# The first products of layer 1 become a kind of their own in the planner of an attention and two-layer kernel

## The chip, the cores and the metric

The kernel runs on one core of one Trainium2 chip. The metric is the device time of one execution in microseconds (us). Three runs of the kernel before took 815.68, 815.87 and 816.68 us; the median is 815.87 us. The traces come from one further, profiled execution.

## The reference

Four batches of eight heads of causal attention over 576 tokens of width 64, with a decay between positions, feed two dense layers over 2304 tokens, all in float32:

```
scores = scale * q @ k.T + (cum[i] - cum[j]),  cum = cumsum(log(clip(f, 1e-4, 1)));  causal
attn   = softmax(scores);   x = attn @ v             # 2304 x 512
h = x @ w_in                                         # layer 1, 512 -> 1024
solu = h * softmax(h);  ln = (solu - mean) / sqrt(var + 1e-6) * g_ln
x = ln @ w_out                                       # 1024 -> 512
h = max(x @ w2_in, 0);  out = (h * h) @ w2_out       # layer 2, 512 -> 2048 -> 512
```

## The kernel before, in words

**Stages.** Attention walks over 20 query tiles (up to 128 rows each, a tile of 64 rows in every batch), and over 8 heads in each. For a head TensorE (PE) makes the scores in a PSUM bank `z` (L567, two matmuls; four for the widest rows, then with both banks), VectorE (DVE) finds the row's least value (L588), ScalarE (ACT) takes the exponential into one of three buffers `adj` (L602), PE transposes it through a rotating PSUM bank `pp` (L621), ACT or DVE copies that to `pt` (L376, L382), and PE multiplies it with `v` into `xo` (L641). When a tile is done its rows are scaled and transposed (L667).

**Layer 1** runs beside attention. Whenever 128 tokens are ready, `first` (L845 on) issues for such a block eight steps of *first products*, three matmuls each: L860, L861, L862, 512 columns, low and high parts of `x` and `w_in`, accumulated in the two banks `hp`. A chain then normalises the block: DVE maximum (L873), ACT exponential (L878), DVE product (L883), ACT square, which overwrites `hp` (L899), POOL scaling into `e` (L921). PE transposes `e` (L938), and `out1` multiplies by `w_out` (L811 to L813). The next block's first products may only write `hp` when L899 is through with it. There are 18 blocks, so 144 such steps. ACT, DVE and POOL also prepare the weights of both layers meanwhile (`convert`, L699 on, and `early2`, L1089 to L1105).

**Layer 2** follows (L1332, L1383, L1484 to L1486), a stretch of dense matmuls that starts at 448.4 us of the span.

**What sets the order.** Nothing is scheduled on the chip: the program's order on each engine is written out by `Plan.lay` (L127 on), a list scheduler that runs when the kernel is built. Each step has a duration per engine, a priority (lower is more urgent) and dependences; `LAT` gives the delay from one engine to another. A step that several engines can do, such as a copy, goes where it ends first. For PE a step also has a *kind*: `r` for ordinary products, `h` for scores of 64 rows, `t` for transposes, `c` for the attention's products with `v`. `TURN` (L48) is the time in ns that the plan adds when PE goes from one kind to another: `tr=86` is from transposes to products. The choice among PE's candidates counts that time, and adds HOLD = 1000 to the priority number of a candidate whose kind is not that of the step before, so that equal kinds stay together. A pair that `TURN` does not list costs nothing. The first products, the products of `out1` and all of layer 2 have the default kind `r`.

**Filler.** Where the plan sees a gap of more than 400 ns on PE before 140 us of its own time (GAP, WARM), it puts in transposes of the identity whose result nobody reads: as many as 60% of the gap takes at 62 ns each (`fill`, L102; `filler`, L1693).

Of the kernel before, what the change touches and what calls it, by code (L numbers as in the profile page):

```python
# [27 lines left out]
class Plan:  # L28
# [10 lines left out]
        pe=dict(pe=0, dve=196, act=215, pool=200, dma=1100),  # L39
# [5 lines left out]

    TICK, DUTY = 10240 / 3, 1280.0

    TURN = dict(rt=20, tr=86, rc=93, tc=94, cr=250, ct=200, th=60, ht=100, rh=20, hr=10, hc=20, ch=200)  # L48

    def __init__(self, slots, banks):  # L50
        self.banks = banks
# [75 lines left out]
    def lay(self, slack=60):  # L127
# [11 lines left out]
        def pe_end(t, ns, mark):  # L139
            k = int(t // self.TICK)  # L140
            while True:
                rate = 1.0 if work.get(k - 1, 0.0) >= self.DUTY else 0.5
                room = max(0.0, (k + 1) * self.TICK - t)
                if ns <= room * rate:
                    if mark:
                        work[k] = work.get(k, 0.0) + ns
                    return t + ns / rate
                if mark:
                    work[k] = work.get(k, 0.0) + room * rate
                ns -= room * rate  # L150
                k += 1
                t = k * self.TICK
# [28 lines left out]
        while todo:  # L181
            pick = None
            for e in engs:
# [21 lines left out]
                if e == "pe":  # L205

                    turn = {x[1]: self.TURN.get(kind + x[1].kind, 0) for x in cand}
                    t0 = min(x[0] + turn[x[1]] for x in cand)
# [37 lines left out]
            if e == "pe":  # L246
                pe_end(t, s.eng[e] + self.TURN.get(kind + s.kind, 0), True)
                kind = s.kind
# [20 lines left out]
def tile_kernel(ctx: ExitStack, tc: tile.TileContext, q, k, v, f, w_in, w_out, g_ln, w2_in, w2_out, out):  # L269
# [8 lines left out]
    KC = DM // P  # L278
# [161 lines left out]
    def slot_time(s):  # L440
        return when[s] if s < len(when) else TEND + (s - len(when)) * 2000
# [403 lines left out]
    def first(x):  # L845

        n0 = xs_done[x]
        a = slot_time(H * (n0 + 1) + LAG)
        b = slot_time(H * (xs_done[x + 1] + 1) + LAG) if x + 1 < NTT else a + EACH * TAILR
        d = b - a  # L850
# [4 lines left out]
        xk = [(nm, i, o) for nm in ("xh", "xl") for o in offs]  # L855
        for c in range(2):
            w = slice(c * 512, c * 512 + 512)
            for cc in range(KC):
                def fn(c=c, cc=cc, w=w):
                    nc.tensor.matmul(HP[:, c], lhsT=XL[i][:, cc, :], rhs=wih[:, cc, w], start=(cc == 0), stop=False)  # L860
                    nc.tensor.matmul(HP[:, c], lhsT=XH[i][:, cc, :], rhs=wil[:, cc, w], start=False, stop=False)  # L861
                    nc.tensor.matmul(HP[:, c], lhsT=XH[i][:, cc, :], rhs=wih[:, cc, w], start=False, stop=(cc == KC - 1))  # L862

                pl.add(
                    dict(pe=693), fn, a + d * FH * (c * KC + cc) / 8, xk + [("wi", cc, c, y) for y in "hl"], ["h"]
                )

        t1 = a + d * FH
# [1 line left out]
        hf = HP.rearrange("p a x -> p (a x)")  # L870
# [118 lines left out]
    def carve(tag, sizes, dt=F32R, old=None):  # L989

        memo = {}
        out, o = [], 0
        for n in sizes:
            def get(o=o, n=n):
                if "t" not in memo:
                    memo["t"] = new(tag, [sum(sizes)], dt)
                return memo["t"][:, o : o + n]

            out.append((get, held[tag] if old is None else old))
            o += n  # L1000
        return out
# [18 lines left out]
    c = carve("woh", [512] * 7 + [256] * 2)  # L1020
# [8 lines left out]
    c = carve("q2", [512] * 4)  # L1029
# [606 lines left out]
    for n in range(NQ):  # L1636
        for h in range(H):
            s = n * H + h
            if h == 0 and n + 2 < NQ:
                load_v(n + 2, when[s])  # L1640
            if h == PK and n + 1 < NQ:
                prep_k(n + 1, when[s])
                if n + 2 < NQ:
                    load_k(n + 2, when[s])
            if h == PQ and n + 1 < NQ:
                prep_q(n + 1, when[s])
                if n + 2 < NQ:
                    load_q(n + 2, when[s])
            head(s)
            w = 4 if n >= QUADS else 2  # L1650
            if (h + 1) % w == 0:
                mix(s, w)
        if tiles[n]["done"]:
            first(tiles[n]["x"])
# [60 lines left out]
FH, FO = 0.25, 0.7  # L1715
# [64 lines left out]
```

## Time and profile before

| what | value |
|---|---|
| median of three runs | 815.87 us |
| the profiled execution | 816.74 us |
| its span, first to last instruction | 814.9 us |
| PE busy | 796.5 us, 98% of the span |
| PE weight loads busy | 730.9 us, 90% |
| DVE, ACT, POOL busy | 636.8, 544.4, 392.2 us |
| DMA | 159.69 MB, 196 GB/s on average |

A busy time is the union of an engine's instructions, and the ends of matmuls are modelled; so PE's work is better read from the distance between the starts of matmuls that follow each other. Filler counts as busy too.

### The profile page before, as it was taken

Reading aid. Unit: us, or ns where it says so; the run is one execution under the profiler, and the core shown is the slowest. Engines: PE = TensorE matmul, PEld = TensorE weight load, DVE = VectorE, ACT = ScalarE, POOL = GpSimd, SP = SyncE. Lnnn points to the kernel's source line nnn. Section 1 sums busy time; section 2 is a strip of 40 time slices with the busy share of each in tenths; the row PEclk is TensorE's granted clock in tenths of the full one; section 3 lists DMA queues with packets and bytes.
Section 4 is the critical chain, followed back from the end, with each engine's and each line's share of the span. In section 5 each row is a group of like instructions: output and inputs, shape, how many; then the busy total and the mean of one; then the engine's idle time right before and its main releaser. Section 6 shows DMA issues by size and latency. Waiting matters only on the chain.

```text
span 814.9 us, 19217 instructions
## 1 busy us (share of the span) xinstructions
PE 796.5 (98%) x6648; PEld 730.9 (90%) x6648; DVE 636.8 (78%) x1626; ACT 544.4 (67%) x1405; POOL 392.2 (48%) x541
## 2 busy tenths in 40 slices
PE   8899999999999999999999999999999999999997
PEld 7677777888888888888889999999999999999997
DVE  8898777878977677677678888789779877987776
ACT  6899988888898888899787765444335433533332
POOL 6467766767678875688767522120211121112110
PEclk9999999999999999999999999999999999999999
DMA  6744336666665455666577899697667767666401
GB/s 198 224 135 131 105 104 189 189 181 198 193 197 192 147 190 172 192 214 197 170 234 245 258 324 371 205 316 228 209 210 240 233 190 245 200 221 189 149 18 36
DMA packets 109665, 159.69 MB, mean 196 GB/s; under 512 B 12832, under 2 KB 52768, under 8 KB 109568
## 3 DMA queue, kind: packets, MB, share of 16 engines
q1 hardware_dynamic: 109568, 158.47, 61.5%
q8 instruction: 52, 0.85, 0.5%
q14 instruction: 45, 0.37, 0.1%
HBM read 121.65 MB, written 36.72 MB: 194 GB/s over the span
## 4 chain that ended last, share of the span: by engine, by line
PE 56%; ACT 3%; DVE 3%; DMA 2%; issue 2%; POOL 1%; DVEq 0%; SPq 0%; POOLq 0%; ACTq 0%
PE z L1383 9%; PE pp L1383 9%; PE hp L1484 3%; PE hp L1486 3%; PE hp L1485 3%; PE z L1332 3%; PE pp L621 2%; PE pp L811 2%; PE z L567 2%; PE xo L1484 2%; PE xo L1486 2%; PE xo L1485 2%; PE pp L812 2%; PE pp L813 2%; PE hp L860 1%
## 5 line engine op out<-in xcount | busy, mean ns | idle before, releaser
L602 ACT ACTIVATE adj<-z,st 64x288 f32<-64x288 f32 (+9 forms) x192 | 95.4, 501 | 17.3 <-DVE st L588 16.4
L567 PE MATMUL z<-k,q 128*128 128x256 f32 (+17 forms) x384 | 89.9, 332 | 0.9 <-ACT adj L602 0.8
L588 DVE CUSTOM_DVE_ANT_0 z<-z,maskb 128x128 f32<-128x128 f32 (+8 forms) x144 | 65.2, 463 | 29.2 <-PE z L567 26.7
L621 PE MATMUL pp<-ident,adj 128*128 128x128 f32 (+1 forms) x480 | 76.2, 274 | 6.1 <-ACT adj L602 4.9
L812 PE MATMUL pp<-ln,wol 128*128 128x256 f32 x288 | 80.2, 278 | 0.0
L813 PE MATMUL pp<-ln,woh 128*128 128x256 f32 x288 | 80.1, 278 | 0.0
L376 ACT COPY pt<-pp 128x256 f32<-128x256 f32 (+5 forms) x169 | 67.4, 420 | 16.5 <-PE pp L621 15.6
L621 PEld LDWEIGHTS pp<-ident,adj 128*128 128x128 f32 (+1 forms) x480 | 50.5, 140 | 30.8 <-ACT adj L602 19.3
L1144 DVE TENSOR_TENSOR k<-adj,k 128x512 fp32r<-128x512 f32 x72 | 50.5, 701 | 32.9 <-POOL k L380 24.9
L380 POOL TENSOR_SCALAR k<-adj 128x512 fp32r<-128x512 f32 x41 | 25.6, 624 | 85.0 <-PE xo L1486 31.7
L734 POOL TENSOR_TENSOR free<-free 128x256 uint32<-128x256 uint32 x64 | 50.4, 794 | 31.0 <-DVE free L728 25.0
L641 PE MATMUL xo<-pt,vn 128*64 128x128 f32 (+1 forms) x960 | 61.3, 268 | 0.6 <-ACT pt L376 0.3
L567 PEld LDWEIGHTS z<-k,q 128*128 128x128 f32 (+3 forms) x384 | 54.8, 177 | 7.6 <-ACT adj L602 3.8
L860 PE MATMUL hp<-wih,xl 128*128 128x512 f32 x144 | 60.3, 419 | 0.8 <-ACT hp L899 0.8
L641 PEld LDWEIGHTS xo<-pt,vn 128*64 128x64 f32 x960 | 49.0, 137 | 11.3 <-issue 6.1
L861 PE MATMUL hp<-wil,xh 128*128 128x512 f32 x144 | 56.6, 393 | 0.2 <-DVE wil L738 0.2
L862 PE MATMUL hp<-wih,xh 128*128 128x512 f32 x144 | 56.7, 393 | 0.0
L812 PEld LDWEIGHTS pp<-ln,wol 128*128 128x128 f32 x288 | 54.4, 189 | 0.5
L813 PEld LDWEIGHTS pp<-ln,woh 128*128 128x128 f32 x288 | 54.2, 188 | 0.0
L1097 POOL TENSOR_TENSOR free<-free 128x256 f32<-128x256 f32 x64 | 51.8, 810 | 3.7 <-DMA w2f<-free 1.2
L1383 PE MATMUL z<-wol,k 128*128 128x256 f32 x384 | 52.5, 276 | 0.0
L1089 POOL TENSOR_TENSOR free<-free 128x256 fp32r<-128x256 f32 x63 | 48.3, 781 | 8.4 <-ACT free L376 7.5
(576 smaller groups left out, 2688.5 us busy)
## 6 DMA issues: line engine op xcount, KB each, us to landing
k<-w2u SPq DMA_DIRECT2D x96, 256.0 KB
ln<-w2u SPq DMA_DIRECT2D x96, 256.0 KB
w2u<-free SPq DMA_DIRECT2D x56, 256.0 KB
kn<-in_k_dram SPq DMA_DIRECT2D x32, 256.0 KB
free<-in_moe_w_out_dram SPq DMA_DIRECT2D x32, 256.0 KB
free<-in_moe_w_in_dram SPq DMA_DIRECT2D x32, 256.0 KB
q<-w2u SPq DMA_DIRECT2D x32, 256.0 KB
w2f<-free SPq DMA_DIRECT2D x49, 128.0 KB
```

The source lines that it names most:

```text
L376: nc.scalar.copy(dst(), src())
L567: nc.tensor.matmul(dst, lhsT=ql[0:r, p, 0:m], rhs=rhs, start=(g == 0), stop=(g == 1))
L588: nc.vector.tensor_tensor_reduce(out=z, in0=z, in1=maskb[0:m, o : o + e - a], scale=1.0, scalar=st[0:m, 0:1] if y else 3e38, op0=ALU.add, ...
L602: nc.scalar.activation(out=adj[0:m, c[1] : c[2]], in_=Z[c[0]][0:m, 0 : c[2] - c[1]], func=AF.Exp, bias=st[0:m, low : low + 1], scale=-1.0, ...
L621: nc.tensor.transpose(at(sk)[:, (c - g) * m : (c - g + 1) * m], adj[0:m, zc : zc + P], ident[0:m, 0:m])
L641: nc.tensor.matmul(XO[own[j], g // 2, off : off + m], lhsT=VN[vslot[b, c]][:, (g + j) * D : (g + j + 1) * D], rhs=PT[(s - h + g + j) % NPT ...
L812: nc.tensor.matmul(px, lhsT=wol[:, fc, w], rhs=hi, start=False, stop=False)
L813: nc.tensor.matmul(px, lhsT=woh[:, fc, w], rhs=hi, start=False, stop=(fc == KF - 1))
L860: nc.tensor.matmul(HP[:, c], lhsT=XL[i][:, cc, :], rhs=wih[:, cc, w], start=(cc == 0), stop=False)
L861: nc.tensor.matmul(HP[:, c], lhsT=XH[i][:, cc, :], rhs=wil[:, cc, w], start=False, stop=False)
L862: nc.tensor.matmul(HP[:, c], lhsT=XH[i][:, cc, :], rhs=wih[:, cc, w], start=False, stop=(cc == KC - 1))
L1383: nc.tensor.matmul(half(i), lhsT=l, rhs=r[:, c * TB : c * TB + TB], start=(j == start), stop=(j == 5), skip_group_check=True,)
```

## The change

`TURN` gets seven pairs with a new kind `f`, and the step of the first products is given that kind. A pair with `f` that is not listed (`fr`) costs nothing. Since these steps are no longer of kind `r`, HOLD now also stands between them and scores, `out1` and layer 2, in both directions.

```
-    TURN = dict(rt=20, tr=86, rc=93, tc=94, cr=250, ct=200, th=60, ht=100, rh=20, hr=10, hc=20, ch=200)
+    TURN = dict(rt=20, tr=86, rc=93, tc=94, cr=250, ct=200, th=60, ht=100, rh=20, hr=10, hc=20, ch=200,
+        rf=85, tf=110, cf=200, hf=85, ft=100, fc=93, fh=20)
...
                 pl.add(
-                    dict(pe=693), fn, a + d * FH * (c * KC + cc) / 8, xk + [("wi", cc, c, y) for y in "hl"], ["h"]
+                    dict(pe=693), fn, a + d * FH * (c * KC + cc) / 8, xk + [("wi", cc, c, y) for y in "hl"], ["h"],
+                    kind="f",
                 )
```

The arithmetic is the same; the built program differs in its order on all five engines. Line numbers of the changed kernel are one or two higher (L860 is L861, L938 is L940). On PE every matmul of the program is there as often as before, except the filler: 256 transposes of the identity before, 225 now. The first 63 rows of PE's order are the same, and after row 2597 of 4238, early in layer 2, nothing differs. Runs of first products without another kind between them are 86 before and 55 now; runs of at least six steps are one before and seven now. Changes between the groups L567 at 128 rows, L567 at 64 rows, transposes, L641, first products, `out1` and layer 2 number 529 before and 484 now.

On PE, in the fifth query tile (64 rows, 576 columns), between two heads. `hp` takes first products, `z` scores, `adj` is transposed for a head, `e` for a block of layer 1. Before:

```order
L621 MATMUL pp_127<-ident_110,adj_26_97 128x64 x5
L567 MATMUL z_122<-k_45_116,q_41_112 64x288
L567 MATMUL z_122<-k_7_78,q_20_91 64x288
L1693 MATMUL pp_126<-ident_110 128x128 x13
L567 MATMUL z_121<-k_45_116,q_41_112 64x288
L567 MATMUL z_121<-k_7_78,q_20_91 64x288
L938 MATMUL pp_126<-ident_110,e_90 128x128 x4
L621 MATMUL pp_125<-ident_110,adj_28_99 128x64 x5
L938 MATMUL pp_127<-ident_110,e_90 128x128 x4
```

The same place in the changed kernel:

```order
L622 MATMUL pp_127<-ident_110,adj_26_97 128x64 x5
L861 MATMUL hp<-wih_74,xl_38_109 128x512
L862 MATMUL hp<-wil_75,xh_37_108 128x512
L863 MATMUL hp<-wih_74,xh_37_108 128x512
L940 MATMUL pp_125<-ident_110,e_90 128x128 x4
L940 MATMUL pp_126<-ident_110,e_90 128x128 x4
L568 MATMUL z_121<-k_45_116,q_41_112 64x288
L568 MATMUL z_121<-k_7_78,q_20_91 64x288
```

The scores of this head stand earlier now, a step of first products and both transposes of `e` stand where 13 filler transposes stood.

On PE, in the fifteenth query tile (64 rows, 576 columns), at the first step of the 13th block of layer 1. `hp` is again the bank of the first products. Before, the transposes of `e` of the 12th block stand ahead of it:

```order
L567 MATMUL z_122<-k_46_117,q_42_113 64x288
L567 MATMUL z_122<-k_8_79,q_20_91 64x288
L621 MATMUL pp_127<-ident_110,adj_28_99 128x64 x5
L938 MATMUL pp_126<-ident_110,e_90 128x128 x4
L938 MATMUL pp_125<-ident_110,e_90 128x128 x4
L860 MATMUL hp<-wih_74,xl_38_109 128x512
L861 MATMUL hp<-wil_75,xh_37_108 128x512
```

The same step in the changed kernel:

```order
L568 MATMUL z_122<-k_46_117,q_42_113 64x288
L568 MATMUL z_122<-k_8_79,q_20_91 64x288
L622 MATMUL pp_126<-ident_110,adj_28_99 128x64 x5
L861 MATMUL hp<-wih_74,xl_38_109 128x512
L862 MATMUL hp<-wil_75,xh_37_108 128x512
```

The block now begins before `e` of the block ahead is transposed. From the last first product of the 12th block to this row PE's order has, in the changed kernel, 20 matmuls of L642 (the trace shows each of this kind twice), transposes of one head, the four score matmuls of a head, 12 products of `out1`, four score matmuls more and the transposes shown.

## Rows read from the trace of the kernel before

**Rows 1.** Windows by stage: busy us (count) of PE, PEld, DVE, ACT, POOL; clock, DMA.

```profile
38.00:88.00 50.00, 47.79 (x351) 37.83 (x351) 41.81 (x95) 48.28 (x118) 34.85 (x45) 1.00 0.44 134
73.80:143.60 69.80, 66.86 (x554) 53.29 (x552) 52.80 (x147) 62.46 (x189) 50.58 (x69) 1.00 0.44 131
143.60:448.40 304.80, 300.34 (x2445) 260.52 (x2444) 228.00 (x601) 261.14 (x735) 221.72 (x299) 1.00 0.62 194
448.40:792.00 343.60, 343.60 (x3014) 343.60 (x3013) 276.83 (x697) 152.70 (x318) 70.89 (x110) 1.00 0.70 225
```

**Rows 2.** Waits of PE in the stretch 143.6 to 448.4: us, times, longest.

```profile
PE pp L621 <- ACT adj L602: 1.9, 6, 0.5
```

**Rows 3.** Timeline of PE, 92 to 101: start, us, instruction; filler, then `out1`.

```profile
94.99 1.58 PE L1693 MATMUL pp<-ident 128*128 128x128 f32 x13
96.44 0.48 PE L567 MATMUL z<-k,q 128*64 128x288 f32 x2
...
100.16 0.28 PE L812 MATMUL pp<-ln,wol 128*128 128x256 f32 x1
...
100.98 0.28 PE L813 MATMUL pp<-ln,woh 128*128 128x256 f32 x1
```

**Rows 4.** Timeline of PE, 112 to 126: changes of kind.

```profile
114.62 0.39 PE L862 MATMUL hp<-wih,xh 128*128 128x512 f32 x1
114.85 0.80 PE L567 MATMUL z<-k,q 128*64 128x288 f32 x4
115.58 0.52 PE L621 MATMUL pp<-ident,adj 64*128 64x64 f32 x5
116.03 0.66 PE L938 MATMUL pp<-ident,e 128*128 128x128 f32 x4
116.44 0.48 PE L860 MATMUL hp<-wih,xl 128*128 128x512 f32 x1
116.76 0.39 PE L861 MATMUL hp<-wil,xh 128*128 128x512 f32 x1
116.99 0.40 PE L862 MATMUL hp<-wih,xh 128*128 128x512 f32 x1
117.31 0.80 PE L641 MATMUL xo<-pt,vn 128*64 128x64 f32 x20
118.05 0.52 PE L621 MATMUL pp<-ident,adj 64*128 64x64 f32 x5
...
118.91 0.78 PE L567 MATMUL z<-k,q 128*64 128x288 f32 x4
119.53 0.39 PE L860 MATMUL hp<-wih,xl 128*128 128x512 f32 x1
```

**Rows 5.** Timeline, 152.6 to 162.7: one block, from last first product to transposes.

```profile
152.81 0.39 PE L862 MATMUL hp<-wih,xh 128*128 128x512 f32 x1
...
157.51 1.21 ACT L899 ACTIVATE hp<-e,sm 128x1024 f32<-128x1024 f32 x1 [0.46 <-DVE sm L893]
...
162.32 0.55 PE L938 MATMUL pp<-ident,e 128*128 128x128 f32 x3 [0.24 <-POOL e L921]
```

**Rows 6.** Timeline, 296 to 301: a head's scores and its transposes.

```profile
296.16 0.71 PE L567 MATMUL z<-k,q 128*128 128x512 f32 x2
...
299.81 0.66 PE L621 MATMUL pp<-ident,adj 128*128 128x128 f32 x4 [0.39 <-ACT adj L602]
```

**Rows 7.** Waits of SP, which issues the DMAs: us, times, longest.

```profile
SPq L1372 <- PE pp L1383: 71.8, 72, 2.8
SPq L1372 <- PE z L1383: 70.9, 71, 2.8
```

**Rows 8.** Windows of PE alone near start and end: busy, clock, DMA share, GB/s.

```profile
2.00:6.00 4.00, 4.00 (x20) 1.00 0.81 266
8.00:10.00 2.00, 2.00 (x21) 1.00 0.48 76
810.00:815.00 5.00, 0.23 (x2) 0.84 0.31 105
```

## The prediction

> **What bounds the kernel now.** I read the windows by stage first. From 448.4 us on PE is busy for 343.60 of 343.60 us, and its order there changes only up to row 2597, early in that stage; so layer 2 costs what it did, and a gain or loss in attention reaches the end whole, if layer 2's inputs come earlier too. In attention there are two regimes [rows 1]. From 38 to 88 us ACT is busy for 48.28 of 50 us: ACT is the bound, and PE, at 47.79, holds filler. From 143.6 to 448.4 us PE is busy for 300.34 of 304.80 us while ACT has 261.14 and DVE 228.00: PE is the bound, and only its matmuls, the changes between their kinds and some 4.5 us of waits count. Next I read PE's waits there, mostly transposes that wait for the exponential: 1.9 us, six times [rows 2]. Last I read the timeline, for what filler and a change of kind cost.
>
> **Filler that goes.** 31 of the 256 filler transposes are gone. 13 of them hold PE from 94.99 until the scores start at 96.44, 1.45 us, with no idle time behind them, so one takes 0.11 us [rows 3]. All 31: 3.4 us. By the order, PE's matmuls without filler up to the first scores of the eighth tile (143.6 us before) are exactly the same ones in both kernels; if PE waits no more than before, it gets there 3.4 us earlier. What decides is ACT. It has 62.46 us of work in the 69.80 from 73.8 to 143.6, and by the order only two instructions more up to that point (277 for 275, shares of the copies moving both ways). In 66.4 us that is 94%, and 38 to 88 us shows that 97% can be held [rows 1]. Nearer in, from the fourth tile's first exponential to the middle of the fifth tile, ACT has 87 instructions for 98 before; the weight preparation that left comes later, where ACT has gaps. So the gaps are really smaller, not only left unfilled. Bounds: the whole 3.4 us comes back, or none, if idle time takes the filler's place. I take -3.4 and +0.6 for new idle time, -2.8.
>
> **Changes of kind.** PE changes 484 times for 529. Changes to or from first products fall by 62: 39 fewer to transposes, 20 fewer from them, 17 fewer from the wide scores, some others more. They are cheap. First products follow each other at 0.23 us. From one to scores it also takes 0.23 (114.62 to 114.85), so nothing. After four transposes, which take 0.41 for 4 x 0.11, the first one takes 0.32: 0.06 for the change. To the products with `v` it takes 0.32, so 0.09 [rows 4]. On the other side there are 18 more changes from wide scores to transposes, and a few others, 17 net; four score matmuls take 0.73 us ahead of transposes and 0.62 ahead of a first product, so 0.11 each, 1.9 us [rows 4]. With 0.03 for one of the 62, nearer the zero of the change to scores, they give back 1.9: together 0. With the ends, 0 and 0.09, it is +1.9 to -3.7. I take -0.2, since the dear changes, those of the products with `v`, become one fewer. The plan's new prices, 100 and 110 ns between first products and transposes, are above what these rows show; they cost no time by themselves, they only choose the order.
>
> **Waits for the exponential.** From the start of a head's scores to its transposes the bare chain takes 3.65 us, with 0.39 of waiting at its end [rows 6]. With the distances of starts as in rows 3 and 4 I added up the PE work that the order puts between a head's last score matmul and its first transposes. From 143.6 us on it is under 2.5 us for 48 of 104 heads before and for 35 now: a step of first products in a run of several covers more. Those waits are 1.9 us there [rows 2]; with a quarter to a half of them gone it is -0.8 (bounds 0 and -1.9).
>
> **A new wait for `hp`.** The 13th block's first products now stand soon behind the 12th's last. From a last first product to the end of the square that frees `hp` it takes 157.51 + 1.21 - 152.81 = 5.91 us [rows 5]. PE's work between in the changed order: 0.32, twice 0.74 less one entry, say 1.3, for 20 products with `v`; 0.45 for a head's transposes; 0.62 and 0.73 for two times four scores; 12 x 0.117 = 1.4 for `out1`; 0.45 again [rows 3, 4]: 5.3 us. PE waits 0.6, and 0.1 for the signal: +0.7. Queued behind it are the next heads' scores; ACT and DVE wait with them. Longer queues on ACT would make it 2.
>
> **The transposes of `e`.** From a block's last first product to these it takes 9.51 us, with 0.24 of waiting [rows 5]. The order leaves under 9 us of matmuls between them in six of 18 blocks (8.06 at least) and in two before; changes of kind add some 0.7 us to such a stretch. So four more waits of 0 to 0.4: +0.5 with a little more for the tightest. Bounds 0 and +2.
>
> **Other engines.** Copies that two engines can do move: 8 of the 72 copies of `out1`'s result from ACT to DVE, some conversions from POOL to ACT and DVE. In 143.6 to 448.4 us DVE idles for 77 us and POOL for 83 [rows 1], which hides them; SP's transfers are the same in number.
>
> **Sum:** -2.8 - 0.2 - 0.8 + 0.7 + 0.5 = -2.6 us. The profiled execution took 816.74 us (its span of 814.9 and 1.8 around it), so 814.1 for it. It lies 0.87 above the median of the runs shown; against that median of 815.87 the forecast is 813.3 us. No change is what differs by at most 0.2%, 1.6 us.
>
> **A rule on the clock, weighed.** From 2 to 6 us of the span only filler runs, and 20 of its transposes start in 4 us; from 8 to 10 us there are 21 in 2 us [rows 8]. PE's pace doubled, as from 1.2 to 2.4 GHz, with nothing but transposes before it. The Trainium skill ("TensorE: Matmul & The Clock Gate", Part 4: PE-mode transpose) says that the full clock doesn't engage for transposes, which don't count as busy in the same way. The trace disagrees; by the page filler holds no clock up and its loss costs none, by the row it could.
>
> **Rivals.**
> 1. *The filler's time stays as idle time.* Then the sum is +0.2: 816.1. For it: ACT is full from 38 to 88 us, and the first scores of the fourth tile come behind four more ACT instructions and five more filler transposes. Or layer 2 eats the gain, because its inputs don't come earlier; against that, SP's loads of its weights wait for PE itself, 143 times, 142.7 us in all [rows 7], so they move with it.
> 2. *Slower: long runs of first products starve ACT.* Runs of six to eight steps (4 to 5.5 us at 0.23 a matmul) are seven now and one before, most of them behind 143.6 us where no filler shows it. During one ACT uses up the two banks of scores; behind it PE has two heads' transposes and scores to do, 2 x (0.45 + 0.62), and then meets a bare chain of 3.65 [rows 4, 6]: 1.5 us for each head so exposed. Six more runs with one head each give +9; if half of that comes, 813.3 + 4.7 = 818. It decides from 4.2 us on, three heads. Against it: the count of heads with little cover falls, as above.
> 3. *More gain:* changes of kind at their cheap end and no new waits: -3.4 - 3.7 + 0.5, about 809.5.
> 4. *The clock falls where filler is gone.* Then matmuls take twice their time for a while, 5 us or more: 818 and above. Against it: it reads below 1.00 only where PE has 0.23 us of work in 5 [rows 8], and from 73.8 to 143.6 us some 61 us of real work are left in 69.8.
>
> **How the numbers follow.** The forecast's own range is 811 to 815, with a chance of 0.55, of which 0.04 lies within 0.2%. Rival 1 has 0.21, of which 0.17 within and 0.04 slower; rival 2 0.15; rival 3 0.06; rival 4 0.03. Faster 0.51 + 0.06 = 0.57, the same 0.21, slower 0.22. The range goes down to 810.2, most of rival 3 left out, and up to 818, half of rivals 2 and 4 left out.
>
> **What would show it.** Right: PE's busy share of 38 to 143 us falls by the filler while the first scores of the eighth tile start near 140.2; layer 2 starts about 446; a wait of PE's first products for the square of 0.5 to 2 us near 320. Wrong: PE's waits between the eighth tile and layer 2 well above 6 us (rival 2), the eighth tile not earlier (rival 1), a clock below 1.00 before 800 us (rival 4).

## The result, and the profile after

The changed kernel took 820.65 us in the median of ten runs (817.56 to 822.87), the kernel before 815.99 us (815.02 to 817.71) on the same chip: a ratio of 1.0052, with a 95% interval of 1.0038 to 1.0067. It is slower by half a per cent; 813.3 us was forecast. The profiled execution of the changed kernel took 819.02 us, 2.28 more than that of before (816.74). L622 is the old L621, L943 the old L941; in the variants below the same lines stand a few numbers higher. Of the runs below, one of k3_before_lessfill (869.03 us) and one of k5_move_fill (2109.9 us) lie far outside the others and are left out of ranges and ratios.

First the windows by stage, which answer to [rows 1], with one of 6.8 us added; columns as there.

```profile
38.00:88.00 50.00, 47.09 (x349) 37.55 (x350) 43.12 (x104) 49.14 (x122) 32.52 (x42) 1.00 0.44 134
73.80:143.60 69.80, 65.66 (x525) 53.44 (x525) 53.12 (x138) 60.38 (x185) 47.67 (x67) 0.95 0.39 119
124.20:131.00 6.80, 6.80 (x48) 5.55 (x49) 3.66 (x11) 3.17 (x11) 2.29 (x4) 0.50 0.60 188
143.60:448.40 304.80, 298.12 (x2433) 261.10 (x2431) 230.46 (x616) 253.70 (x709) 223.65 (x303) 1.00 0.60 193
448.40:792.00 343.60, 343.60 (x3014) 343.60 (x3012) 278.34 (x699) 158.75 (x332) 66.80 (x106) 1.00 0.70 227
```

Layer 2 is as full as before. The second row is the one to look at: the granted clock is 0.95 where it was 1.00, and the third row shows why. For 6.8 us it is 0.50, so 1.2 instead of 2.4 GHz, with PE busy all the time: 48 matmuls run there, in the same window of the kernel before 68. Such a stretch at 0.50 is called a fall from here on.

Now the timeline of PE just ahead of that window: start, us, instruction, and in brackets the idle time ahead of it and what ended it.

```profile
120.61 0.52 PE L622 MATMUL pp<-ident,adj 64*128 64x64 f32 x5
123.00 0.27 PE L622 MATMUL pp<-ident,adj 64*128 64x64 f32 x1 [1.87 <-DVE ln1b L943]
...
128.09 0.41 PE L813 MATMUL pp<-ln,wol 128*128 128x256 f32 x1
128.31 0.41 PE L814 MATMUL pp<-ln,woh 128*128 128x256 f32 x1
...
132.06 0.28 PE L812 MATMUL pp<-ln1a,woh 128*128 128x256 f32 x1
132.17 0.28 PE L813 MATMUL pp<-ln,wol 128*128 128x256 f32 x1
```

PE waits 1.87 us for a `pp` bank, the longest wait of the whole program behind its first microseconds. From 124.2 on matmuls of `out1` start 0.21 to 0.22 us apart, and 0.11 us again behind 131. The bank is freed by VectorE's L943. This is VectorE's timeline there, then GpSimd's:

```profile
118.70 3.52 DVE L533 SCALAR_TENSOR_TENSOR q<-qn,q 64x512 fp32r<-64x512 f32 x1
122.25 0.69 DVE L943 TENSOR_TENSOR ln1b<-pp,ln 128x512 fp32r<-128x512 f32 x1
```

```profile
118.85 3.96 POOL L735 TENSOR_TENSOR free<-free 128x256 uint32<-128x256 uint32 x5
```

L533 is a step of 0.69 us (the median of its forty). This one takes 3.52, while GpSimd adds five pieces of a weight back to back; L943 stands behind it. Before, there was nothing longer than a row of three here.

The planner had kept the two apart. VectorE's steps with `port=True`, L533 among them, are laid where GpSimd is idle (`lay` waits for `free["pool"]`). In the changed kernel's plan, by its own time, L533 stands from 113.20 to 113.80 us: GpSimd's step for `k` (L497) ends at 113.20, the first of the five additions starts at 113.80, and PE has no gap from 112.6 to 121 us. But only the order on each engine and the data's dependences go into the program. In the trace GpSimd goes straight on at 118.85, and L533, begun at 118.70 while L497 still ran, is caught.

The waits of PE in 143.6 to 448.4 us (us, times, longest), for [rows 2]:

```profile
PE pp L622 <- ACT adj L603: 2.1, 5, 1.0
PE hp L861 <- ACT hp L901: 1.2, 2, 1.0
PE z L568 <- ACT adj L603: 0.8, 2, 0.6
PE pp L622 <- DVE ln1b L943: 0.7, 1, 0.7
```

The waits for the exponential did not shrink (1.9 before), and two are new. The second row holds the predicted one: in the timeline it stands at 323.16, with the square that ends it, to be set against [rows 5]:

```profile
321.68 1.21 ACT L901 ACTIVATE hp<-e,sm 128x1024 f32<-128x1024 f32 x1 [0.23 <-DVE sm L895]
```

```profile
323.16 0.47 PE L861 MATMUL hp<-wih,xl 128*128 128x512 f32 x1 [1.02 <-ACT hp L901]
```

### The profile page after: what moved, and what is told of

The parts are those of the page before. It is cut to its first block, busy times and chain, and to the rows that moved or that the text cites. A ratio compares the mean times of both kernels' runs of the same rounds, so it can differ in the third digit from the quotient of the medians.

```text
span 817.2 us, 19145 instructions
## 1 busy us (share of the span) xinstructions
PE 792.5 (97%) x6617; PEld 730.6 (89%) x6617; DVE 640.6 (78%) x1642; ACT 543.2 (66%) x1396; POOL 383.7 (47%) x534
## 5 line engine op out<-in xcount | busy, mean ns | idle before, releaser
L622 PE MATMUL pp<-ident,adj 128*128 128x128 f32 (+1 forms) x480 | 73.2, 272 | 9.5 <-ACT adj L603 6.4
L377 ACT COPY pt<-pp 128x384 f32<-128x384 f32 (+5 forms) x164 | 64.6, 421 | 19.1 <-PE pp L622 18.2
L622 PEld LDWEIGHTS pp<-ident,adj 128*128 128x128 f32 (+1 forms) x480 | 51.1, 141 | 25.2 <-ACT adj L603 14.5
L735 POOL TENSOR_TENSOR free<-free 128x256 uint32<-128x256 uint32 x64 | 52.4, 826 | 28.6 <-DVE free L729 18.0
L642 PE MATMUL xo<-pt,vn 128*64 128x128 f32 (+1 forms) x960 | 60.7, 271 | 0.8 <-ACT pt L377 0.4
L861 PE MATMUL hp<-wih,xl 128*128 128x512 f32 x144 | 58.8, 408 | 2.0 <-ACT hp L901 1.4
L642 PEld LDWEIGHTS xo<-pt,vn 128*64 128x64 f32 x960 | 49.0, 139 | 11.0 <-issue 6.0
```

The source lines that it names most:

```text
L377: nc.scalar.copy(dst(), src())
L622: nc.tensor.transpose(at(sk)[:, (c - g) * m : (c - g + 1) * m], adj[0:m, zc : zc + P], ident[0:m, 0:m])
L642: nc.tensor.matmul(XO[own[j], g // 2, off : off + m], lhsT=VN[vslot[b, c]][:, (g + j) * D : (g + j + 1) * D], rhs=PT[(s - h + g + j) % NPT ...
```

## The experiments

Eleven variants and one repetition. Each ratio is to runs of the kernel before measured beside the variant on the same chip (medians of 816.7 to 817.0 us). Clocks are means over a run; of 88 such runs of the kernel before, 75 have 0.998 to 1.000. In its profile only the idle end is at the half clock.

### Does the time go with the clock?

The changed kernel once more.

> The changed kernel once more, for a second trace and for the clock of each run. Theory: its time goes with how long TensorE's clock is at half: runs with a mean granted clock of 0.996 to 0.997 take 817.5 to 820 us, runs with 0.990 to 0.992 take 821 to 823, and a second trace with a lower mean shows a second stretch at half clock beside the one at 124 us. Rival (the time comes from new waits alone): the times do not sort by the clock.

Measured: 823.78 us in the median of seven (816.63 to 827.40), ratio 1.0079 (1.0050 to 1.0107). Over both sets its runs sort by clock: 816.63 at 0.998, 817.6 to 820.1 at 0.996 to 0.997, 821.2 to 822.9 at 0.990 to 0.992, 822.5 to 823.9 at 0.988, 826.2 to 827.4 at 0.982. The profiled run (821.73 us) has the half clock at 124.3 for 6.8 us, behind the same wait of 1.9 us, and at 325.7 for 3.4 us, behind the wait for `hp`. So nearly all that the changed kernel loses goes with the clock. The one run with a whole clock takes what before takes (816.63 us), not less.

### Take the wait away: VectorE's order

```diff
+ order.remove(marks["ql", 6, 1])                                  # L533
+ order.insert(order.index(marks["lnl", 2, 1]) + 1, marks["ql", 6, 1])  # behind L943
```

> One DVE instruction is moved behind the subtraction that frees the pp bank (L943); all other engines keep their order word for word. Theory: the 1.87 us wait of PE at 123.0 us is gone, because the instruction that was held up 2.8 us by five POOL instructions no longer stands ahead of L943; without that wait the clock does not fall at 124 us (which cost 3 us or more), so the median is 814 to 817 us and the mean clock 0.998 or 0.999. Rival 1 (the wait matters, the clock does not): 1.9 us less, 818.8. Rival 2 (long runs of first products and the new waits behind 143 us cost the time): no change, 820.6.

Measured: 817.27 us (814.64 to 819.25), ratio 1.0006 (0.9995 to 1.0016). The median is 3.4 us below the first set of runs of the changed kernel and 6.5 below the second. The wait at 123 us and the fall behind it are gone from the profile, as this window shows:

```profile
120.00:140.00 20.00, 18.97 (x160) 14.94 (x158) 15.07 (x45) 15.30 (x58) 13.85 (x19) 1.00 0.58 184
```

The profiled run (819.25 us) fell at 321.1 for 6.8 us, which I had not expected. PE's timeline:

```profile
318.39 0.52 PE L623 MATMUL pp<-ident,adj 64*128 64x64 f32 x5
319.94 0.47 PE L862 MATMUL hp<-wih,xl 128*128 128x512 f32 x1 [1.02 <-ACT hp L902]
...
323.56 0.63 PE L864 MATMUL hp<-wih,xh 128*128 128x512 f32 x1
323.99 0.63 PE L862 MATMUL hp<-wih,xl 128*128 128x512 f32 x1
```

Behind the predicted wait, 1.02 us, stands a second fall: first products start 0.43 apart instead of 0.23.

### Keep the wait, fill it

The changed order as it is, with 17 transposes in the wait at 123 us:

```diff
+ if s == 39:
+     for _ in range(17):
+         nc.tensor.transpose(at(sk)[:, 384:512], ident, ident)
```

> 17 filler transposes (1.85 us) are put where PE waits 1.87 us, into columns of the pp bank that nobody reads; everything else keeps its order. Theory: the wait's time stays, but PE does not stand idle, and the clock does not fall at 124 us: 816.5 to 818.5 us, mean clock 0.998 or more. Rival 1 (transposes do not hold the clock up): the half-clock stretch stays, 820.6 or a little more. Rival 2 (the clock does not matter): 820.6.

Measured: 818.61 us (817.10 to 821.12), ratio 1.0024 (1.0014 to 1.0034). PE's timeline and a window of its profiled run (817.10 us):

```profile
121.11 2.08 PE L625 MATMUL pp<-ident 128*128 128x128 f32 x17
123.11 0.27 PE L622 MATMUL pp<-ident,adj 64*128 64x64 f32 x1
```

```profile
120.00:140.00 20.00, 19.18 (x165) 15.35 (x165) 14.88 (x44) 14.15 (x55) 12.67 (x18) 1.00 0.56 173
```

Real work is held up as long as in the changed kernel (it resumes at 123.11 for 123.00), and VectorE's L533 takes 3.53 us as before; only the emptiness is gone, and the clock stays at 1.00. So in this profile it is the empty wait that costs the clock, not the delay. The median lies 1.3 us above k1_move's, of which the wait itself may be most; runs with clocks down to 0.993 show that falls elsewhere remain, though no profile of this variant shows where.

### Filler alone, in the old order

The kernel before, its filler ended at 80 us (`WARM` 80000 instead of 140000; 29 transposes fewer).

> The kernel before with 227 instead of 256 filler transposes: the last three groups (13, 6 and 10) are left out, all other instructions keep their order. If the filler by itself keeps the clock up there, the clock falls somewhere between 90 and 140 us in this kernel too: 818 to 821 us, mean clock 0.997 or less. If only a wait of PE of about 2 us, which the kernel before does not have there, lets it fall: 816, clock 0.999, no change.

Measured: 816.27 us, ratio 0.9990 (0.9974 to 1.0007), clocks of 0.997 to 1.000. So the loss of this filler alone does not move the median. That it never costs the clock is not shown. The only profile is that of the run of 869.03 us, so it is no more than a hint, but where 13 transposes had been, PE waits 1.29 us in it for an exponential (until 98.46), and the half clock stands right behind, at 99.2 for 3.4 us.

### A long wait, in the old order

The kernel before, with one of VectorE's steps (old L941, for the third block) carried out seven times.

```diff
+ if (x, g) == (2, 1):
+     ls.fn = lambda lo=lo: [lo() for _ in range(7)]
```

> The kernel before, in its own order, with one step repeated: VectorE's subtraction for ln1b of the third block (near 121 us), which frees a pp bank, is carried out seven times instead of once, with the same result, so that the bank comes free 4 us later. Theory: TensorE waits 1 to 3 us for the bank near 123 us, and its clock falls for some 7 us behind it as in the changed kernel, though the order is the old one: 3.4 us for the clock on top of the wait, median 819.5 to 823, mean clock 0.990 to 0.995. Rival 1: the clock falls only in the new order (its mix of work), and the old one bears the wait: 817 to 819.5, clock 0.998 or more. Rival 2: TensorE has slack there and waits under 0.5 us: 816 to 817, and the run says nothing.

Measured: 826.31 us (824.68 to 827.71), ratio 1.0113 (1.0089 to 1.0137), clocks of 0.985 to 0.991. PE's timeline, and the window of the fall:

```profile
126.87 0.68 PE L667 MATMUL pp<-ident,x 64*128 64x64 f32 x4 [3.10 <-ACT x L376]
```

```profile
124.70:148.60 23.90, 21.73 (x116) 18.03 (x117) 13.62 (x47) 13.04 (x48) 6.71 (x10) 0.50 0.38 116
```

The old order falls too, so the new kind is not needed for it; a long wait is enough. The wait is not for the bank, as I had expected, but for `x`, whose scale stands behind the repeated step on VectorE. The fall begins at 124.7, 0.9 us into the wait, and lasts 23.9 us, not 7, so the time came out above my range; why it lasts so much longer is not settled. That the repeated step delays other engines as well is a rival that the next run was to settle.

### The same wait with filler: a miss

k7_before_wait, with 27 transposes ahead of L667.

> k7_before_wait, the kernel before with the repeated step that makes TensorE wait 3.1 us at 126.9 us, and nothing changed but 27 filler transposes put into that wait, in a bank that is free. The wait is as long, only not empty. Theory (the empty wait makes the clock fall, and the fall is the larger price): no stretch below 1.00 between 100 and 160 us, where k7_before_wait had 23.9 us at half, and a median of 816.5 to 819.5, 7 to 10 below its 826.31. Rival: the fall comes from the delay of the other engines or of real matmuls, and transposes don't count for the clock; then the half-clock stretch stays and the median is 825 to 828.

Measured: 823.96 us (821.46 to 825.99), ratio 1.0081 (1.0056 to 1.0106), clocks of 0.997 to 0.999. The bank I chose was not free, as PE's timeline shows:

```profile
125.91 4.83 PE L1697 MATMUL pp<-ident 128*128 128x128 f32 x27 [2.16 <-DVE ln1b L942]
130.67 0.46 PE L668 MATMUL pp<-ident,x 64*128 64x64 f32 x4
```

The filler waits for the very step that was slowed, and then holds real work up to 130.67. So this is no test of a filled wait, and the rival of k7_before_wait stays open. It shows two things all the same. The clock fell behind the 2.16 us and was back after 3.4 us, at 130.0, while nothing but transposes ran:

```profile
126.60:130.00 3.40, 3.40 (x18) 3.40 (x17) 0.63 (x1) 1.12 (x6) 0.00 (x0) 0.50 0.26 77
130.00:150.00 20.00, 19.27 (x172) 15.71 (x170) 13.82 (x48) 15.61 (x57) 10.96 (x15) 1.00 0.55 172
```

And that wait and that filler in the profile, 2.16 + 4.83 = 6.99 us, are about the 7.28 us by which its median lies above before.

### What held VectorE up

The changed kernel; of GpSimd's five additions three are moved behind the next four short steps.

```diff
+ for y in pool[run + 2 : run + 5]:
+     order.remove(y)
+ order[at9:at9] = pool[run + 2 : run + 5]
```

> The changed kernel, only GpSimd's order changed: of the five 128x256 additions back to back at 118.85 us the last three come after the next five short steps. Theory: VectorE's 64x512 multiplication for q is held up by that run of GpSimd's, as long as it lasts; with two of five left it takes 1.5 to 2.3 us instead of 3.52, TensorE's wait at 123 us shrinks from 1.87 to under 0.5 us and the clock does not fall there. Median as k1_move, 816.0 to 817.6. Rival: the multiplication is slow for a reason of its own, stays at 3.5 us, and the time is that of the changed kernel, 819.5 to 824.

Measured: 816.60 us (814.66 to 819.10), ratio 0.9981 (0.9959 to 1.0003). VectorE's timeline, GpSimd's, and the window behind:

```profile
118.77 1.43 DVE L533 SCALAR_TENSOR_TENSOR q<-qn,q 64x512 fp32r<-64x512 f32 x1
```

```profile
118.92 1.89 POOL L735 TENSOR_TENSOR free<-free 128x256 uint32<-128x256 uint32 x2
```

```profile
120.00:140.00 20.00, 18.93 (x164) 15.18 (x163) 14.15 (x46) 16.00 (x60) 14.71 (x20) 1.00 0.62 193
```

With two additions (118.92 to 120.81) it takes 1.43 us, with five 3.52. The wait and the fall at 123 us are gone; the fall behind the wait for `hp` (319.4, for 6.8 us) is there. Of its six runs with a clock of 0.998 or more, four took 814.7 to 815.3 us and two 816.5 and 816.8; the four hint at what the change could be worth.

### Both falls mended

k1_move, with nine transposes in the wait for `hp`, in the bank of the head that was just transposed:

> The changed kernel with VectorE's multiplication for q behind its subtraction for ln1b (as in k1_move), and nine filler transposes at the end of the step of head transposes ahead of the first product that waits 1.02 us for hp near 320 us. Theory: the time goes with TensorE's clock, the clock falls behind a wait of about 1 us or more in dense work, and transposes in that wait hold it up. Then no stretch below 1.00 behind 320 us in the profile, a mean clock of 0.998 or more in most runs, and a median of about 815 us (814.3 to 816.0), 2 below k1_move's 817.27, below the kernel before. Rival: falls come anywhere, whatever TensorE waits for; then the median stays at 816.8 to 817.8 with clocks of 0.994 to 0.998 in half of the runs.

Measured: 816.52 us (815.64 to 817.51), ratio 0.9991 (0.9976 to 1.0006), all clocks at 0.998 or more. The clock held, but the copy out of that bank now waited for the filler, and the next scores waited behind it. VectorE's timeline, then PE's:

```profile
319.81 0.49 DVE L384 COPY pt<-pp 128x320 f32<-128x320 f32 x1 [1.30 <-PE pp L1707]
```

```profile
321.52 0.95 PE L569 MATMUL z<-k,q 128*64 128x288 f32 x4 [0.93 <-ACT adj L604]
```

The changed order with both waits filled in this manner:

> The changed kernel in its own order, with 17 filler transposes in the 1.87 us wait at 123 us (as in k2_gapfill) and nine in the 1.02 us wait near 320 us: both waits stay, only their emptiness goes. Theory: mean clock 0.998 or more in nearly all runs, median 816.4 to 817.6, 1 to 2 below k2_gapfill's 818.61 and 1.5 to 2.5 above k5_move_fill, which is the price of the wait at 123 us itself. Rival (falls anywhere): median 818 to 819 as k2_gapfill, clocks down to 0.993.

Measured: 818.21 us (817.25 to 820.99), ratio 1.0013 (0.9995 to 1.0030). Clocks are 0.998 or more in 11 of 12 runs, as the theory has it, but the median is above its range and inside the rival's; the delay that this filler makes is in it, since PE waits 0.93 us for an exponential here too (until 324.72). The rival is not idle either: the profiled run fell once elsewhere, at 98.2 for 3.4 us, behind two waits of 0.5 and 0.4 us and where the changed plan has no filler any more.

Then the nine transposes in an idle third bank, on k1_move and on k9_poolsplit:

```diff
+ def held_clock(f=first12.fn, i=min(idle)[1]):
+     filler(i, 9)
+     f()
+ first12.fn = held_clock
```

> As k5_move_fill, only the nine transposes write a third, idle pp bank instead of the bank of the head that was just transposed, so that the copy out of that bank need not wait for them. In k5_move_fill the fall near 320 us was gone, but the next scores waited 0.93 us for an exponential. Theory: that wait came from the held-up copy and goes; the clock stays whole: median 814.5 to 815.6, 1 to 2 below k5_move_fill's 816.52, ratio to the kernel before about 0.998. Rival: the wait for the exponential is there whatever bank is written, and the median stays at 816 to 817.

> k9_poolsplit (GpSimd's five additions parted, no wait at 123 us) with the same nine transposes in the idle bank near 320 us. k9_poolsplit took 814.66 to 815.26 where the clock stayed at 0.998 or more and 816.4 to 819.1 where not. Theory: nearly all runs now lie at 814.4 to 815.5, the ratio to the kernel before is 0.997 to 0.9985, and the changed order beats the old one. Rival: falls at other places take the place of this one, and the median stays at 816 to 817.

Measured: 815.35 us (814.69 to 817.67), ratio 0.9980 (0.9963 to 0.9997), and 815.21 us (814.56 to 816.03), ratio 0.9976 (0.9959 to 0.9992). Both are below both kernels, by 0.2% against the one before. PE's timeline of k11_split_free:

```profile
317.93 1.20 PE L1696 MATMUL pp<-ident 128*128 128x128 f32 x9
319.01 0.47 PE L862 MATMUL hp<-wih,xl 128*128 128x512 f32 x1
319.32 0.40 PE L863 MATMUL hp<-wil,xh 128*128 128x512 f32 x1
319.56 0.40 PE L864 MATMUL hp<-wih,xh 128*128 128x512 f32 x1
319.80 0.91 PE L569 MATMUL z<-k,q 128*64 128x288 f32 x4
```

The scores come without a wait, and first products start 0.24 apart.

### Other prices for the new kind

```diff
- rf=85, tf=110, cf=200, hf=85, ft=100, fc=93, fh=20
+ rf=0, tf=60, cf=200, hf=0, ft=60, fc=90, fh=0
```

> The changed kernel with other prices for the new kind, near what the matmuls show: nothing between scores and first products (85 and 20 before), 60 ns for transposes to first products (110) and back (100), 90 to the products with v (93). The plan makes another order. Theory: the changes of kind decide nothing (within 1 us); what decides is whether the new order happens to hold waits of 1 us or more behind which the clock falls. Without them 814 to 816.5 at a clock of 0.998 or more, with one or two of them 818 to 823 at 0.990 to 0.996. Rival: truer prices by themselves gain, 812 to 813.5.

Measured: 817.78 us (816.51 to 818.71), ratio 1.0006 (0.9990 to 1.0021), clocks of 0.999 to 1.000. Truer prices gain no time; but this plan is slower than my 816.5 without a fall. Parted as in the table below, its profile has the lowest rest of all (752.2 us), which speaks for cheaper changes of kind, but 14.4 us of idle time and 23.5 of filler, which take that back. The head transposes wait longer for the exponential than in any of the other profiles, 3.1 us where before has 1.9 [rows 2]; waits of PE, 143.6 to 448.4 us:

```profile
PE pp L622 <- ACT adj L603: 3.1, 5, 1.0
PE z L568 <- ACT adj L603: 1.0, 3, 0.4
PE pp L622 <- ACT pt L377: 0.8, 1, 0.8
```

One wait of 1.05 us (at 232.0) brought no fall here. Which waits do is open.

## Why the prediction was wrong

The table parts the time of the profiled executions up to PE's last matmul into `hp`, which layer 2 uses too, in us. Idle time is what PE is not busy from 13.5 us on; filler, from there on too, is the distance from the start of each filler transpose to that of the next matmul, less idle time; the clock is half of the stretches at 0.50; the rest, matmuls and changes of kind, is what is left (up to 0.3 us of its differences is the start, where the 13th product comes at 14.1 to 14.4 us).

| | before | changed | k2_gapfill | k11_split_free |
|---|---|---|---|---|
| last matmul into `hp` | 788.55 | 790.86 | 788.47 | 786.19 |
| idle | 10.92 | 15.66 | 13.75 | 12.77 |
| filler | 22.10 | 18.75 | 20.78 | 19.95 |
| clock | 0 | 3.41 | 0 | 0 |
| rest | 755.54 | 753.03 | 753.94 | 753.47 |

- **Filler** (-3.4): right, 22.10 less 18.75 is 3.35. It was won, too: the sixth tile's first scores come at 116.9 us for 121.7. Between there and the seventh tile it was lost.
- **Changes of kind** (-0.2): too small. The rest falls by 1.6 to 2.1 in the four new-order profiles without a fall (k2, k5, k10, k11); it is inside the bounds of +1.9 and -3.7, and my choice near zero was not. With a fall in it the rest (2.51 here) is less sure, since PE is not the bound at half pace.
- **New wait for `hp`** (+0.7): right in place and size, 1.02 us at 323. The 0.1 us for the signal stood on no row; here PE starts 0.27 us behind the square's end (321.68 + 1.21 to 323.16). That the wait could cost the clock as well was not in the sum.
- **Waits for the exponential and for `e`** (-0.8 and +0.5): the first did not come (2.1 us for 1.9), the second hardly (0.3 us for 0.2). Idle time as a whole rose by 4.74, where my terms make +1.0. The largest part is the 1.87 us at 123.
- **Together:** +4.74 of idle time, -3.35 of filler, +3.41 for the clock and -2.51 for the rest make the 2.3 us by which the changed profile lies behind. Its median lies further off (820.65 us), since five of its ten runs have clocks of 0.990 to 0.992, the profiled one 0.996; k0_again's profile shows a second fall.
- **The failed step** is the sentence "if PE waits no more than before, it gets there 3.4 us earlier". PE waited 1.87 us more at one place, and the half clock behind it cost another 3.4 us, more than the whole gain. I weighed only ACT as what might make PE wait. I had compared VectorE's and GpSimd's instructions by their number and idle time, not by what runs beside what: a 0.69 us step behind which a bank hangs came to lie beside five of GpSimd's. The plan's own times would have shown L533 between two of GpSimd's steps with nothing to hold it there. And I had rival 4 bound to lost filler, at 0.03, with the argument that PE is busy for 61 us in 69.8. An average over 70 us says nothing on one empty stretch of 1.9. Its price, 5 us or more, stood on no row; one fall of 6.8 us costs 3.4. In its own form, a fall where filler is gone, it shows in one profile, k6_bothfill's at 98.2.
- **The other rivals:** PE's waits between the eighth tile and layer 2 rose from 4.5 to 6.7 us, half of the 4.2 from which rival 2 was to decide. Layer 2 starts at 448.0 us, not 446.

In the table k2_gapfill ends level with before: -1.6 for the rest, -3.35 for filler, +2.83 for idle time and +2.03 for the filler put into the wait. (The parts add up by construction, since the rest is what is left.) k11_split_free shows the forecast's path when both waits are dealt with: the eighth tile's first scores at 139.9 us (140.2 forecast, 143.6 before, 144.3 in the changed kernel), and 815.21 us for 816.68, 1.5 us less where 2.6 were forecast.

On the rule that I weighed: the clock column of [rows 8] reads 1.00 in both windows, so those rows speak by PE's pace alone. k2_gapfill (the clock stays at 1.00 over the filled wait) and k12_wait_filled (it comes back while only transposes run) say it more plainly: transposes do hold the clock up. The Trainium skill ("TensorE: Matmul & The Clock Gate", Part 4: PE-mode transpose) says they don't count as busy in the same way; no run here bears that out.

## What to carry to other kernels

When a new order is judged, look for the one long wait that it makes, not at sums of busy time: on a full engine an empty stretch of 1 to 2 us cost up to 3.4 us more by the clock behind it. A plan's times are no promise: what it keeps apart on two engines stays apart only if a dependence, or each engine's own order, holds it there. Where such a wait can't be scheduled away, fill it with transposes in a bank that no one waits for and that is free; in a bank with a reader the same nine gave about half of their gain back (ratios of 0.9991 for 0.9980, with 1.0006 without them; the intervals overlap, and the mechanism is in the timelines). For each step behind which a bank hangs, ask what GpSimd can come to do beside it.

## What the hardware showed that I had not expected

- **VectorE held up by GpSimd.** L533, with both inputs in SBUF, takes 0.69 us alone, 1.43 beside two of GpSimd's additions back to back and 3.52 beside five; in k1_move, started at 120.52 beside the end of the same five, 2.01. Each time it ends 0.6 us before the end of the row (122.22 of 122.81, 120.20 of 120.81, 122.53 of 123.13), and the last addition of each row takes 1.18 to 1.20 us where the others take 0.73 to 0.76: VectorE got in ahead of the last one, and not before. L943, which reads PSUM, takes its usual 0.69 us beside them in k1_move. The Trainium skill ("SBUF — State Buffer", SBUF: two separate sides) tells of a lock on a pair of ports that VectorE and GpSimd share, held for one whole instruction. The rows agree that one of the two is held up by the other; but here VectorE did not get in behind the first instruction of GpSimd's that ended, so the price was that of the row less its last one.
- **The clock.** It fell behind waits of 1.87 us (124.2, 6.8 us long), 1.02 (321.1 and 319.4, 6.8; 325.7, 3.4) and 2.16 (126.6, 3.4), in one of 3.10 us (124.7, 23.9), and once behind no more than 0.5 and 0.4 us (98.2, 3.4). It did not fall behind the same 1.02 us in the changed kernel's own profile (323.16), nor behind 1.34 us at 29 us in the kernel before. The length of a wait alone does not decide. The kernel before is not safe from it either: 13 of the 88 runs of it beside the variants took 820.4 to 824.1 us at clocks of 0.990 to 0.993; no profile shows where it fell in them.
